# A row tile transposed inside the first Q tile, copied out by two engines, and the second Q tile put ahead of the first K tile

## Chip, cores, metric

One core of one Trainium2 chip. The metric is the device time of one execution in microseconds (us). A run is called fast or slow by its granted clock and its time; only fast runs are compared here.

## The reference

Sequence 2048, width 512. One layer norm feeds two branches that are added to the input: a sliding dilated attention with 32 heads of 16, a window of 8 and a dilation of 2, and a gated feed-forward of inner width 1376.

```python
def _A_ref(x, wqkv, wo):
    ...
    qkv = (lambda x, *d: x.transpose(*d))((x @ wqkv).reshape(B, S, 3, H, Dh), 2, 0, 3, 1, 4)
    ...
    idx = pos[:, None] - off[None, :]          # off = 0, 2, ..., 14
    ...
    logits = jnp.einsum("bhsd,bhswd->bhsw", q, kg) * scale
    logits = jnp.where(mask[None, None, :, :], logits, -1e9)
    attn = _softmax(logits, axis=-1)
    o = jnp.einsum("bhsw,bhswd->bhsd", attn, vg)
    return (lambda x, *d: x.transpose(*d))(o, 0, 2, 1, 3).reshape(B, S, D) @ wo

def _B_ref(x, w_gate, w_up, w_down):
    g = jnp.einsum("bsd,df->bsf", x, w_gate)
    u = jnp.einsum("bsd,df->bsf", x, w_up)
    h = _gelu(g) * u
    return jnp.einsum("bsf,fd->bsd", h, w_down)

xn = _layernorm(x, axis=-1)
return x + _A_ref(xn, A_wqkv, A_wo) + _B_ref(xn, B_w_gate, B_w_up, B_w_down)
```

## The kernel before

The kernel lists every piece of work as a task with an engine, a modelled duration, what it reads and writes, and a priority. A list scheduler written into the kernel then fixes the order on each engine, the buffers and the semaphore waits. So a change of one priority can move instructions everywhere. The sequence is cut into four blocks of 512 rows, each of four row tiles of 128.

Priorities are shifted by group of tasks, and two constants say how much slack the scheduler leaves for TensorE:

```python
SHIFT = {
    "acc0": 361, "acc1": -284, "acc3": -893, "er1": 381, "er2": 159, "er3": -18, "ffn0": 449, "ffn1": -216,
    # ... 30 more
}
SCHED = dict(PE_SLACK=1.6, DMA_BPUS=250e3,
             TOL=dict(pe=0.6, act=-0.3, dve=-0.3, pool=-0.3, sp=0.0))
```

The weights of Q, K and V come in three transfers on the same queue as the input tiles, in the order of their priorities:

```python
t_w = G.task("sp", "ld_w" + nm, 0, mk(), wr=[(I_wq, nm)],
             prio=(-958, -957.5, -898)[i], nbytes=512 * 1024)      # i = q, k, v
```

In block 0 each normalised row tile is transposed by TensorE (`tpx`) and copied out of PSUM. Tile 0 alone is split over two PSUM buffers and copied out by ScalarE (`evx`) and VectorE (`evy`) at the same time (from 5.50 and 5.53 us in the trace); the others are copied by ScalarE alone:

```python
it_tp = Item("tpx" + nm, P_ps, "tp")
it_t2 = Item("tpy" + nm, P_ps, "tp") if nm == "0_0" else it_tp
# ... transposes into it_tp and it_t2
if p == 0 and grp[0] == 0:
    def mk_ev2(it=it_t2, itx=XTI[b], o=o):
        return lambda e: e.tensor_copy(
            out=xnT[:, itx.slot, 2:4, o:o + 128],
            in_=PSB[:, 1024 * it.slot + 256:1024 * it.slot + 512].rearrange("q (k c) -> q k c", k=2))
    t_of["evy" + nm] = G.task("dve", "evy" + nm, d_dve(256), mk_ev2(), rd=[it_t2],
                              wr=[(XTI[b], ("y", p % 2, grp[0]))], prio=-200)
nk = 2 if "evy" + nm in t_of else 4
# ... evx copies the first nk of 4 quarters on ScalarE
```

The Q (`mmt0_t`) and K (`mmt1_t`) tiles of block 0 are 16 matmuls of 128 columns each. Their order on TensorE, and that of VectorE's layer norm steps, is fixed by hand:

```python
chain(["bnst0", "bnag0", "sub0", "rstd0", "norm0", "bnst1", "bnag1", "evy0_0", "sub1", "rstd1", "norm1",
       "bnst2", "bnag2", "sub2", "rstd2", "norm2", "bnst3", "bnag3", "sub3", "rstd3", "norm3", "bnst4"])
# ...
chain(warm_tasks[:len(WARM[0])] + ["tpx0_0"] + warm_tasks[len(WARM[0]):] +
      ["mmt0_0", "tpx0_1", "mmt1_0", "mmt0_1", "tpx1_0", "mmt1_1", "tpx1_1",
       "mmt0_2", "mmt1_2", "mmt0_3", "mmt1_3"])
```

`warm_tasks` are matmuls on zeros that keep TensorE busy while the first tile is normalised (11 in the trace, from 1.25 us on, the last two after tile 0's transposes). After Q, K and V of block 0 (V: 16 matmuls of 512 columns), the attention's elementwise products run on VectorE, and TensorE sums them with narrow, column-tiled matmuls. The logits task `er` begins with 8 matmuls in tiles of 64 columns (the last columns of the up projection) and goes on in tiles of 32 columns; the output sums `pvr` are in tiles of 32 columns alone:

```python
def mk_r(grp=list(er_grp), lg=it_lg, itu=it_u10, itx=XTI[b]):        # er
    def f(e):
        for kt in range(4):
            for c in range(2):
                ins = e.matmul(PS[64 * c:64 * c + 64, ...], lhsT=Wt[:, kt, 128:192], rhs=xnT[...],
                               start=(kt == 0), stop=(kt == 3), tile_position=(0, 64 * c))
        for (g, prs) in grp:
            for wq in range(2):
                for sj in range(4):
                    ins = e.matmul(PS[32 * sj:32 * sj + 32, ...], lhsT=E8[...], rhs=UNI[...],
                                   start=(g == 0), stop=(g == 3), tile_position=(0, 32 * sj))
# ...
                    ins = e.matmul(PS[32 * d4:32 * d4 + 32, ...], lhsT=E4[:, :], rhs=UNI[...],   # pvr
                                   start=(half == 0), stop=(half == 1), tile_position=(0, 32 * d4))
```

Everything else (feed-forward, output projection, accumulation) is ordinary matmuls of 128 to 512 columns.

Of the kernel before, what the change touches and what calls it, by code (L numbers as in the profile page):

```python
# [11 lines left out]
    TOL=dict(pe=0.6, act=-0.3, dve=0.0, pool=0.0, sp=0.0),  # L12
    DMA_ISSUE=0.48,
    DMA_FIXED=2.0,
    DMA_BPUS=330e3,
    ACT_SWITCH=1.35,
    PE_SLACK=0.0,
# [128 lines left out]
class Graph:  # L146
# [466 lines left out]
    def report(self):  # L613
# [11 lines left out]


SHIFT = {
    "acc0": 361, "acc1": -284, "acc3": -893, "er1": 381, "er2": 159, "er3": -18, "ffn0": 449, "ffn1": -216,
    "ffn2": 73, "ffn3": -40, "fin0": -21, "fin1": 305, "fin2": 27, "fin3": -492, "h0": -6, "h1": -944,
    "h2": 606, "ldb1": 326, "ldb2": -35, "ln1": -1581, "ln2": 55, "prod0": 440, "prod1": 888, "prod3": -18,  # L630
    "pv1": -412, "pv2": 970, "pvr0": -976, "pvr1": 126, "pvr2": 463, "qkv1": -43, "qkv2": -1147, "qkv3": -216,
    "sm1": -57, "sm2": -519, "sm3": 750,
}
SCHED = dict(PE_SLACK=1.6, DMA_BPUS=250e3,
             TOL=dict(pe=0.6, act=-0.3, dve=-0.3, pool=-0.3, sp=0.0))

GROUPS = ((r"(?:bnst|bnag|ve|sq|rstd|sub|norm)(\d+)$", "ln", 4), (r"trx(\d+)", "ln", 2),
          (r"(?:mm|evq|evk|evv|stv)(\d)_", "qkv", 1), (r"pr(\d)_", "prod", 1), (r"er(\d)_", "er", 1),
# [29 lines left out]
def bass_parallel_sum__sliding_local_dilated__glu_gated_geglu__prompt_kernel(nc, A_x, A_wqkv, A_wo, B_x, B_w_gate, B_w_up, B_w_down, out, dbg=None, cfg=None):  # L668
# [41 lines left out]
    with contextlib.ExitStack() as es:  # L710
        block = es.enter_context(nc.Block())

        def sb(name, shape, dt):
# [50 lines left out]
        G = Graph()  # L764
        P_ps = Pool("ps", 8, psum=True, quotas=QUOTAS)
# [17 lines left out]
        I_wq = Item("Wqkv")  # L783
# [35 lines left out]
               rd=[I_cf], wr=[I_ident], prio=PC)  # L819
# [10 lines left out]
               rd=[I_E8f], wr=[I_E8], prio=PC2)  # L830
        G.task("pool", "c_zpad", 0.1, lambda e: e.memset(zpad[:, :], 0.0), wr=[I_zpad], prio=PC2)
        G.task("pool", "c_ktpad", 0.15, lambda e: e.memset(KT[:, KTI[0].slot, :, 0:16], 0.0), wr=[(KTI[0], "pad")],
               prio=PC2)
# [9 lines left out]
               rd=[I_E4f], wr=[I_E4], prio=PC2)  # L843
# [4 lines left out]
            rd=[I_mask], wr=[I_mask], prio=PC2 + 10)  # L848
        G.task("act", "c_tbl", 1.5, lambda e: e.activation(
            out=onef[:, 1:2], in_=onef[:, 0:1], func=ACTF.Sqrt),  # L850
            rd=[(I_onef, 0)], wr=[(I_onef, 1)], prio=PC, table="sqrt")
# [3 lines left out]
            rd=[I_zpad], wr=[(I_VD, "pad")], prio=PC + 100, nbytes=512 * 32)  # L855
# [14 lines left out]
        for i, nm in enumerate(("q", "k", "v")):  # L870
            def mk(i=i):
# [4 lines left out]
                         prio=(-958, -957.5, -898)[i], nbytes=512 * 1024)  # L876
# [8 lines left out]
        for (i, src, c0, c1, o) in ((0, B_w_gate, 1280, 1376, 32), (1, B_w_up, 1280, 1312, 0),  # L885
# [9 lines left out]
            wr=[(I_wd, 0)], prio=R_WD, nbytes=1280 * 1024)  # L895
# [13 lines left out]
        t_of = {}  # L909
        XTI = [Item("xt%d" % b, P_xt, "x") for b in range(NB)]  # L910
        for p in range(NP):
# [5 lines left out]
            if p < 2:  # L917
                for t2 in range(2):
                    def mk_ld(t2=t2, p=p, it=it_x):
# [3 lines left out]
                                 prio=((-960, -959), (-957.8, -956.5))[p][t2], nbytes=128 * 1024)  # L923
# [83 lines left out]
            for grp in ((0,), (1,)):  # L1007
                n = len(grp)
                nm = "%d_%d" % (p, grp[0])
                it_tp = Item("tpx" + nm, P_ps, "tp")  # L1010
                it_t2 = Item("tpy" + nm, P_ps, "tp") if nm == "0_0" else it_tp

                def mk_tp(it=it_tp, it2=it_t2, ito=it_x, grp=grp, n=n):
                    def f(e):
                        ins = None
                        for q, t2 in enumerate(grp):
                            for kt in range(4):
                                c0 = 1024 * (it, it2)[kt // 2].slot + kt * 128 * n + q * 128
                                ins = e.transpose(PSB[:, c0:c0 + 128], XIN[:, ito.slot, t2, kt * 128:(kt + 1) * 128],
                                                  ident[:, :])  # L1020
                        return ins
                    return f
                t_tp = G.task("pe", "tpx" + nm, d_mm(128, 4 * n), mk_tp(), rd=[(it_x, t2) for t2 in grp] + [I_ident],
                       wr=[it_tp] if it_t2 is it_tp else [it_tp, it_t2], prio=(-200 if b == 0 else base + 4), mode="f", util=0.5)

                t_tp.urgent = b == 0

                o = 256 * (p % 2) + 128 * grp[0]
                if p == 0 and grp[0] == 0:
                    def mk_ev2(it=it_t2, itx=XTI[b], o=o):  # L1030
                        return lambda e: e.tensor_copy(
                            out=xnT[:, itx.slot, 2:4, o:o + 128],
# [5 lines that stand above are left out]
                def mk_ev(it=it_tp, itx=XTI[b], n=n, o=o, nk=nk):  # L1038
                    return lambda e: e.activation(
                        out=xnT[:, itx.slot, 0:nk, o:o + 128 * n],  # L1040
                        in_=PSB[:, 1024 * it.slot:1024 * it.slot + 128 * nk * n].rearrange("q (k c) -> q k c", k=nk),
                        func=ACTF.Identity)
                t_ev = G.task("act", "evx" + nm, d_act(128 * nk * n), mk_ev(), rd=[it_tp],
                              wr=[(XTI[b], (p % 2, t2)) for t2 in grp], prio=(-200 if b == 0 else base + 6))
                t_of["evx" + nm] = t_ev
                t_of["tpx" + nm] = t_tp
        def chain(names):
            ts = [t_of[q] if isinstance(q, str) else q for q in names]
            for q0, q1 in zip(ts, ts[1:]):
                G.order_after(q1, q0)  # L1050

        chain(["bnst0", "bnag0", "sub0", "rstd0", "norm0", "bnst1", "bnag1", "evy0_0", "sub1", "rstd1", "norm1",
               "bnst2", "bnag2", "sub2", "rstd2", "norm2", "bnst3", "bnag3", "sub3", "rstd3", "norm3", "bnst4"])
        chain(["norm3", "bnst5"])
        chain(["evx0_0", "sq1"])

        QTI = []
        for b in range(NB):
# [7 lines left out]
            if b == 0:  # L1066
                lead = []
                for t in range(4):
                    for which in range(2):
                        it_mm = Item("mmt%d_%d" % (which, t), P_ps, "qkv")  # L1070

                        def mk_mm(which=which, t=t, it=it_mm, itx=XTI[0]):
                            def f(e):
                                ins = None
                                for g in range(4):
                                    for kt in range(4):
                                        ins = e.matmul(  # L1077
                                            PS[:, 512 * it.slot + 128 * g:512 * it.slot + 128 * g + 128],
                                            lhsT=Wqkv[:, kt, which * 512 + g * 128:which * 512 + (g + 1) * 128],
                                            rhs=xnT[:, itx.slot, kt, t * 128:(t + 1) * 128],  # L1080
                                            start=(kt == 0), stop=(kt == 3))
                                return ins
                            return f
                        t_mm = G.task("pe", "mmt%d_%d" % (which, t), 16 * 0.0563, mk_mm(),
                                      rd=[(XTI[0], (t // 2, t % 2)), (I_wq, "qk"[which])]
                                      + ([(XTI[0], ("y", 0, 0))] if t == 0 else []), wr=[it_mm],
                                      prio=-100 + t, mode="f")
                        t_mm.urgent = True
                        t_of["mmt%d_%d" % (which, t)] = t_mm

                        def mk_e(which=which, t=t, it=it_mm, itq=it_qt):
                            def f(e):
                                if which == 0:
                                    o = QT[:, itq.slot, :, t * 128:(t + 1) * 128]
                                else:
                                    o = KT[:, KTI[0].slot, :, 16 + t * 128:16 + (t + 1) * 128]
                                return e.activation(
                                    out=o, in_=PS[:, 512 * it.slot:512 * it.slot + 512].rearrange(
                                        "q (g c) -> q g c", g=4), func=ACTF.Identity)
                            return f  # L1100
                        t_of["ev%s0_%d" % ("qk"[which], t)] = G.task("act", "ev%s0_%d" % ("qk"[which], t), d_act(512), mk_e(), rd=[it_mm],
                               wr=[(it_qt, ("t", t)) if which == 0 else (KTI[0], ("t", t))], prio=-100 + t)
                chain(["evk0_0", "sq3"])
                chain(warm_tasks[:len(WARM[0])] + ["tpx0_0"] + warm_tasks[len(WARM[0]):] +
                      ["mmt0_0", "tpx0_1", "mmt1_0", "mmt0_1", "tpx1_0", "mmt1_1", "tpx1_1",
                       "mmt0_2", "mmt1_2", "mmt0_3", "mmt1_3"])
            for hf in range(nh):
                xparts = [XTI[b]] if nh == 1 else [(XTI[b], (hf, 0)), (XTI[b], (hf, 1))]
                hb = base + (10 * hf if nh > 1 else 0)
# [414 lines left out]
```

## Time and profile before

| | before |
|---|---|
| time, median of 3 runs | 196.44 us (196.17 to 196.82) |
| span of the profiled run | 194.6 us |
| TensorE, VectorE, ScalarE busy | 97%, 79%, 53% |
| V of block 0 starts | 14.53 us |
| first feed-forward matmul | 17.99 us |
| last group of matmuls starts | 191.35 us |

The last three rows are how I read this kernel.

TensorE has no real wait between the V stage and the end, so the time falls into two parts that can be compared apart: **the start** (until V) and **the rest** (first feed-forward matmul to the last group: 191.35 - 17.99 = 173.36). In the views of time shown below, each line has start, duration, engine, line of the kernel, operation, what it writes and reads, and in square brackets the idle time before it and what ended that. A group whose count is one short (15 for 16) has a record missing at its front: 0.22 us of a 512-column matmul are then taken off its start.

### The profile page before, as it was taken

How to read it: one execution, taken by the hardware profiler on the slowest of the kernel's cores; microseconds unless marked ns; L12 is line 12 of the kernel's file. 1: busy time of each engine (PE TensorE's matmuls, PEld its weight loads, DVE VectorE, ACT ScalarE, POOL GpSimd, SP SyncE). 2: the span in 40 equal slices, each digit the busy share in tenths (PEclk: the TensorE clock that was granted, in tenths of full speed). 3: DMA queues.
4: the chain of work that ended last, by engine and by line, in shares of the span. 5: the costliest groups of instructions: out<-in, count | busy, mean ns of one | idle time of the engine just before them, and what ended most of it. 6: DMA issues, size and time to landing. Idle time of an engine off the chain costs nothing.

```text
span 194.6 us, 3228 instructions
## 1 busy us (share of the span) xinstructions
PE 188.5 (97%) x1205; PEld 91.1 (47%) x1224; DVE 153.6 (79%) x240; ACT 104.1 (53%) x171; POOL 8.5 (4%) x31
## 2 busy tenths in 40 slices
PE   7899999999999999999999999999999999999994
PEld 2794444444444443444434444444444444344484
DVE  5989978999799999998999866998974619972132
ACT  3577583776973679701457701764679006586000
POOL 6011001001000000001000100000000000000000
DMA  5999998998723853063657454014970440010121
GB/s 141 352 398 315 312 169 183 263 193 208 185 57 82 220 141 83 18 167 106 162 157 195 58 136 135 27 45 123 245 185 3 108 136 27 0 59 0 44 77 40
DMA packets 34799, 27.03 MB, mean 139 GB/s; under 512 B 11264, under 2 KB 33248, under 8 KB 34784
## 3 DMA queue, kind: packets, MB, share of 16 engines
q1 hardware_dynamic: 34784, 26.83, 54.1%
q8 instruction: 9, 0.15, 0.4%
q14 instruction: 6, 0.05, 0.1%
HBM read 19.99 MB, written 5.26 MB: 130 GB/s over the span
## 4 chain that ended last, share of the span: by engine, by line
PE 81%; DVE 8%; issue 3%; ACT 3%; DMA 3%; SPq 1%; DVEq 0%; ACTq 0%
PE PS L1360 29%; PE PS L1439 19%; PE PS L1123 13%; PE PS L1435 7%; DVE UNI L1308 4%; PE PS L1329 3%; PE PS L1077 3%; PE PS L1207 3%; DMA Wqkv<-in_A_wqkv_dram 3%; PE PS L1395 1%; DVE UNI L1177 1%; ACT UU L1377 1%; PE PS L1200 1%; DVE HT L1382 1%; DVE HT L1410 1%
## 5 line engine op out<-in xcount | busy, mean ns | idle before, releaser
L1439 PE MATMUL PS<-Wd,HT 128*128 128x512 bf16 (+2 forms) x205 | 40.8, 345 | 0.2
L1360 PE MATMUL PS<-xnT,Wu 128*128 128x512 bf16 x154 | 39.6, 379 | 0.6 <-issue 0.5
L1360 PE MATMUL PS<-xnT,Wg 128*128 128x512 bf16 x156 | 39.4, 379 | 0.4 <-issue 0.3
L1308 DVE TENSOR_TENSOR UNI<-BS,PT 128x2048 bf16<-128x2048 bf16 x32 | 37.1, 1219 | 2.9 <-DMA XR<-in_A_x_dram 1.8
L1177 DVE TENSOR_TENSOR UNI<-QT,KT 128x2048 bf16<-128x2048 bf16 x32 | 37.1, 1218 | 0.2
L1377 ACT ACTIVATE UU<-PS 128x512 bf16<-128x512 f32 x40 | 24.0, 601 | 21.2 <-PE PS L1360 21.1
L1123 PE MATMUL PS<-xnT,Wqkv 128*128 128x512 bf16 x155 | 34.8, 379 | 0.5 <-DVE PS L1245 0.2
L1370 ACT ACTIVATE GG<-PS 128x512 bf16<-128x512 f32 x40 | 23.8, 602 | 18.2 <-PE PS L1360 18.1
L1439 PEld LDWEIGHTS PS<-Wd,HT 128*128 128x128 bf16 x209 | 19.6, 98 | 18.5
L1459 DVE TENSOR_TENSOR OB<-PS,XR 128x512 bf16<-128x512 f32 (+2 forms) x19 | 11.5, 605 | 18.3 <-PE PS L1439 18.3
L1360 PEld LDWEIGHTS PS<-xnT,Wg 128*128 128x128 bf16 x160 | 15.3, 98 | 19.6 <-ACT UU L1377 0.8
L1360 PEld LDWEIGHTS PS<-xnT,Wu 128*128 128x128 bf16 x160 | 15.3, 98 | 19.6 <-issue 0.8
L1123 PEld LDWEIGHTS PS<-xnT,Wqkv 128*128 128x128 bf16 x160 | 15.4, 98 | 19.2 <-issue 0.8
L1382 DVE TENSOR_TENSOR HT<-GG,UU 128x512 bf16<-128x512 bf16 x40 | 15.8, 421 | 9.5 <-ACT UU L1377 9.4
L1435 PE MATMUL PS<-Wo,OT 128*128 128x512 bf16 (+2 forms) x76 | 16.9, 345 | 0.1
L1133 ACT ACTIVATE QT<-PS 128x512 bf16<-128x512 f32 x12 | 7.2, 597 | 15.4 <-PE PS L1123 15.4
L1340 ACT ACTIVATE OT<-PS 128x512 bf16<-128x512 f32 x16 | 8.7, 594 | 5.9 <-PE PS L1329 5.8
L1147 ACT ACTIVATE VT<-PS 128x512 bf16<-128x512 f32 x16 | 9.6, 597 | 4.1 <-PE PS L1123 4.1
L937 DVE BATCH_NORM_STATS2 st<-XIN 128x6 f32<-128x512 bf16 x16 | 10.4, 682 | 1.2 <-DMA XIN<-in_A_x_dram 1.2
L1435 PEld LDWEIGHTS PS<-Wo,OT 128*128 128x128 bf16 x76 | 7.2, 98 | 7.0
L1140 ACT ACTIVATE KT<-PS 128x512 bf16<-128x512 f32 x12 | 7.2, 598 | 2.9 <-PE PS L1123 2.9
L1077 PE MATMUL PS<-xnT,Wqkv 128*128 128x128 bf16 x128 | 7.8, 219 | 0.6 <-DMA Wqkv<-in_A_wqkv_dram 0.5
(63 smaller groups left out, 130.9 us busy)
## 6 DMA issues: line engine op xcount, KB each, us to landing
BS<-vt_scratch SPq DMA_DIRECT2D x64, 128.5 KB, 3.0
vt_scratch<-VT SPq DMA_DIRECT2D x16, 128.0 KB
XR<-in_A_x_dram SPq DMA_DIRECT2D x16, 128.0 KB, 2.1
out_dram<-OB SPq DMA_DIRECT2D x14, 128.0 KB, 2.0
Wqkv<-in_A_wqkv_dram SPq DMA_DIRECT2D x3, 512.0 KB, 4.2
XIN<-in_A_x_dram SPq DMA_DIRECT2D x6, 256.0 KB, 7.9
Wg<-in_B_w_gate_dram SPq DMA_DIRECT2D x1, 1280.0 KB
Wu<-in_B_w_up_dram SPq DMA_DIRECT2D x1, 1280.0 KB
```

Of the source, the lines that this page charges most:

```text
L937: return lambda e: e.bn_stats(out=st[:, t, :], in_=XIN[:, it.slot, t2, :])
L1077: ins = e.matmul(PS[:, 512 * it.slot + 128 * g:512 * it.slot + 128 * g + 128], lhsT=Wqkv[:, kt, which * 512 + g * 128:which * 512 + (g + 1 ...
L1123: ins = e.matmul(PS[:, 512 * it.slot:512 * it.slot + HWD], lhsT=lhsT, rhs=xnT[:, itx.slot, kt, c0:c0 + HWD], start=(kt == 0), stop=(kt == 3))
L1177: return lambda e: e.tensor_tensor(out=UNI[:, it.slot, :, :], in0=bass.AP(QT, (itq.slot * 4 + g) * 512, [[NQT * 4 * 512, 128], [0, 4], [1, ...
L1308: return lambda e: e.tensor_tensor(out=bass.AP(UNI, ito.slot * 2048, [[NUNI * 2048, 128], [512, 4], [128, 4], [1, 128]]), in0=bass.AP(BS, ...
L1360: ins = e.matmul(PS[0:M, 512 * it.slot:512 * it.slot + 512], lhsT=Wx[:, kt, j * 128:j * 128 + M], rhs=xnT[:, itx.slot, kt, :], start=(kt = ...
L1370: return lambda e: e.activation(out=GG[0:M, ito.slot, :], in_=PS[0:M, 512 * it.slot:512 * it.slot + 512], func=ACTF.Gelu_apprx_tanh)
L1377: return lambda e: e.activation(out=UU[0:M, ito.slot, :], in_=PS[0:M, 512 * it.slot:512 * it.slot + 512], func=ACTF.Identity)
L1382: return lambda e: e.tensor_tensor(out=HT[0:M, ito.slot, j, :], in0=GG[0:M, ig.slot, :], in1=UU[0:M, iu.slot, :], op=ALU.mult)
L1435: ins = e.matmul(PS[:, 512 * it.slot:512 * it.slot + CW], lhsT=OT[:, ito.slot, dq, ti * 128:(ti + 1) * 128], rhs=Wo[:, dq, c0:c1], start=( ...
L1439: ins = e.matmul(PS[:, 512 * it.slot:512 * it.slot + CW], lhsT=HT[:, ith.slot, j, ti * 128:(ti + 1) * 128], rhs=Wd[:, j, c0:c1], start=Fal ...
L1459: return lambda e: e.tensor_tensor(out=OB[:, ito.slot, 0:CW], in0=PS[:, 512 * it.slot:512 * it.slot + CW], in1=XR[:, itx.slot, c0:c1], op= ...
```

## The change

The intent is to take away TensorE's wait on the K weights: put the Q tile of row tile 1 ahead of the K tile of row tile 0, have tile 1 ready sooner by transposing it inside the first Q tile (after 12 of its 16 matmuls), and shorten its copy-out by giving half to VectorE. All priorities were then tuned anew.

```diff
 SHIFT = {
-    "acc0": 361, "acc1": -284, "acc3": -893, "er1": 381, ...
+    "acc0": 91, "acc2": 150, "acc3": 165, "er0": -90, ...
 }
-SCHED = dict(PE_SLACK=1.6, DMA_BPUS=250e3,
-             TOL=dict(pe=0.6, act=-0.3, dve=-0.3, pool=-0.3, sp=0.0))
+SCHED = dict(PE_SLACK=1.0, DMA_BPUS=250e3,
+             TOL=dict(pe=0.3, act=-0.3, dve=-0.3, pool=-0.3, sp=0.0))
...
-                it_t2 = Item("tpy" + nm, P_ps, "tp") if nm == "0_0" else it_tp
+                it_t2 = Item("tpy" + nm, P_ps, "tp") if p == 0 else it_tp
...
-                if p == 0 and grp[0] == 0:
+                if p == 0:
...
-               "bnst2", "bnag2", "sub2", "rstd2", "norm2", ...
+               "evy0_1", "bnst2", "bnag2", "sub2", "rstd2", "norm2", ...
...
+                        gs = (0, 1, 2, 3)
+                        if t == 0 and which == 0:
+                            t_mm = G.task("pe", "mma0_0", 12 * 0.0563, mk_mm((0, 1, 2)), rd=mrd, wr=[it_mm],
+                                          prio=-100, mode="f")
+                            ...
+                            gs = (3,)
...
-                chain(["evk0_0", "sq3"])
+                chain(["evx0_0", "sq1", "evx0_1", "evq0_0", "sq2"])
+                chain(["evx1_0", "sq3"])
                 chain(warm_tasks[:len(WARM[0])] + ["tpx0_0"] + warm_tasks[len(WARM[0]):] +
-                      ["mmt0_0", "tpx0_1", "mmt1_0", "mmt0_1", "tpx1_0", "mmt1_1", "tpx1_1",
-                       "mmt0_2", "mmt1_2", "mmt0_3", "mmt1_3"])
+                      ["mma0_0", "tpx0_1", "mmt0_0", "mmt0_1", "mmt1_0", "tpx1_0", "mmt1_1", "mmt0_2", "tpx1_1",
+                       "mmt1_2", "mmt0_3", "mmt1_3"])
```

## The prediction

No term of its sum is among them: it still comes to 0.0 for the start, the middle and the end each, 196.4 us. 0.38 and 0.58 to 0.60 us are ScalarE's copies of 256 and 512 columns in the trace, and 0.16 us is the time from the end of a copy to the start of the Q matmul. That a reordering makes no matmul cheaper was the assumption (0.0558 us for 128 columns and 0.863 for a group of four of 512, in the kernel before).

> **What bounds the kernel now.** I read the page first, then the list of waits of TensorE, then the timeline of the first 26 us, then the timelines of TensorE and VectorE over the rest.
>
> From the page of the kernel before, the span and the busy time of each engine:
>
> ```profile
> span 194.6 us, 3228 instructions
> ...
> PE 188.5 (97%) x1205; PEld 91.1 (47%) x1224; DVE 153.6 (79%) x240; ACT 104.1 (53%) x171; POOL 8.5 (4%) x31
> ```
>
> TensorE (PE) is busy almost throughout. The list of waits of TensorE alone (columns: who waited for whom, total us, times, longest) says how little there is to win:
>
> ```profile
> PE PS L863 <- DVE wsrc L812: 1.2, 1, 1.2
> PE PS L1360 <- issue: 0.8, 5, 0.2
> PE PS L1077 <- DMA Wqkv<-in_A_wqkv_dram: 0.5, 1, 0.5
> PE PS L1123 <- DVE PS L1245: 0.2, 1, 0.2
> PE PS L1123 <- issue: 0.2, 1, 0.2
> ```
>
> The first is the start of the program. The only other real wait is 0.5 us for the K weights. The 0.2 us pieces are each one missing record: where they stand, a group of four shows only three matmuls (0.16 us is less than one 0.216 us matmul). The timeline of the start (start, duration, engine, line, operation) shows where the 0.5 us lies:
>
> ```profile
> 4.86 0.61 PE L1019 MATMUL PS<-ident,XIN 128*128 128x128 bf16 x4
> ...
> 5.50 0.38 ACT L1039 ACTIVATE xnT<-PS 128x256 bf16<-128x256 bf16 x1 [1.34 <-PE PS L1019]
> 5.53 0.26 DVE L1031 COPY xnT<-PS 128x256 bf16<-128x256 bf16 x1
> ...
> 6.04 1.05 PE L1077 MATMUL PS<-xnT,Wqkv 128*128 128x128 bf16 x16
> ...
> 6.30 0.35 DVE L993 TENSOR_SCALAR XIN<-XIN,rstd 128x512 bf16<-128x512 bf16 x1
> 6.57 0.69 DVE L937 BATCH_NORM_STATS2 st<-XIN 128x6 f32<-128x512 bf16 x1
> ...
> 6.93 0.39 PE L1019 MATMUL PS<-ident,XIN 128*128 128x128 bf16 x4
> ...
> 7.71 0.58 ACT L1039 ACTIVATE xnT<-PS 128x512 bf16<-128x512 bf16 x1
> ...
> 7.83 1.96 PE L1077 MATMUL PS<-xnT,Wqkv 128*128 128x128 bf16 x32 [0.51 <-DMA Wqkv<-in_A_wqkv_dram]
> ...
> 14.75 3.40 PE L1123 MATMUL PS<-xnT,Wqkv 128*128 128x512 bf16 x15
> ```
>
> The reader is to see: row tile 0 is transposed at 4.86 and copied out of PSUM in two halves (ScalarE 5.50, VectorE 5.53); its Q tile runs at 6.04; tile 1 is transposed at 6.93; then TensorE stands until the K weights land, 7.83. The V stage shows 15 of 16 records, so it began one matmul earlier, 14.75 - 0.22 = 14.53. From 7.83 to 14.53 are 6.70 us for 112 matmuls and 8 transposes of 128 columns, 0.0558 each: no hidden stall in there. From 14.53 to the last matmul (191.35 + 0.78 = 192.13) TensorE has no gap. So the bound is TensorE's own work, plus 6 us of start and about 2.5 us of end.
>
> [...] the trace has 0.38 and 0.58 to 0.60. So halving a copy-out saves ScalarE about 0.2 us, not half. [...] the trace has it between 5.88 (copy ends) and 6.04 (Q matmul starts): 0.16 us, and I charge that for each hand-over from a copy to TensorE.
>
> **The change part by part.** (a) Only 12 of tile 0's 16 Q matmuls precede tile 1's transpose, the other 4 follow. (b) Tile 1's transpose is copied out by ScalarE and VectorE in halves. (c) Tile 1's Q goes before tile 0's K, so the K weights are needed one tile later. (d) The small square roots on ScalarE and the VectorE order are rechained. (e) All priorities and two slack constants are retuned, so the whole schedule is another one. No matmul is added or removed.
>
> Start, with the trace's durations. Nothing before 6.04 changes. Twelve matmuls end at 6.04 + 12 x 0.056 = 6.71; tile 1 is normalised at 6.65, so its transpose starts at 6.75. A copy starts 0.43 after its transpose (10.05 against 9.62 for tile 2), so at 7.18; the half copies end at 7.56 (ScalarE, 0.38) and 7.44. Q of tile 1 may start at 7.56 + 0.16, about 7.70. Meanwhile TensorE does the transpose and the 4 leftover matmuls: 6.75 + 8 x 0.056 = 7.20. So it stands for about **0.45 to 0.5 us**, where it stood 0.51 before: the wait on the K weights (they land near 7.8, needed now near 8.6) becomes a wait on tile 1's copy-out. The restart at 7.70 instead of 7.83 is worth 0.13.
>
> It is given back. VectorE now does tile 1's copy at 7.18 to 7.44 before tile 2's statistics, which started at 6.57: its chain is 0.85 us later. Tile 2 took 1.82 us from statistics to normalised (6.57 to 8.39), so it is ready at 9.25; its transpose comes at 7.70 + 32 x 0.056 = 9.49: just in time. Its copy-out (a full 0.60) runs 9.92 to 10.52, released 10.68; TensorE has one K tile between, done at 9.49 + 20 x 0.056 = 10.61: 0.07 lost. The same distance comes again at tile 3: 0.07. Sum: 7.70 + 6.70 + 0.14 = 14.54 against **14.53** before. The start gains nothing, with perhaps 0.2 us either way.
>
> Middle: the order of instructions shows the same matmuls. Each change between full-array and column-tiled matmuls (L1207, L1329) costs about 0.22 us (0.10 in; out, 98.56 to 99.54 is 0.98 for 0.86 of work). Both orders have 11 such excursions: before, the last logits pass was merged with an output sum; after, the second logits pass is. So nothing there. The question is only whether TensorE now has to wait. VectorE's deadlines, with a 2048-column product at 1.146 us (9.16 for 8) and a 4-matmul group at 0.863:
> - first logits: products start 0.9 later (18.0, not 17.12) and end at 27.2; TensorE arrives two groups sooner, 14.53 + 3.45 + 12 x 0.863 + 0.1 = 28.4. Spare 1.2.
> - second logits: the last product ends near 63 (block 1's products start near 46 after the softmax of block 0 and the normalisation of block 2, with copies of the gated product and four attention products in between), TensorE is there near 67.5: about 4 us spare. Third and fourth: one group sooner than before; about 1.2 each.
> - output sums of blocks 0 to 2: 0.6 to 1.7 spare, worked likewise.
> - output sums of block 3: VectorE starts 0.91 after the accumulations end, as before (160.33 to 161.24); TensorE comes after 7 groups (6.04) where 0.91 + 4 x 1.146 = 5.49 is needed, and again at 6.04 + 1.1 + 3.45 = 10.6 against 10.07. Spare 0.4 to 0.5, the tightest; before it was 168.19 - 165.8 = 2.4 and 171.87 - 170.4 = 1.5.
>
> ScalarE has the same 10 table loads. The end (three half tiles, two quarter tiles) is the same.
>
> Sum: start 0.0, middle 0.0, end 0.0: **196.4 us**.
>
> **The rivals.** First, the wait removed is really gone: if copy-out and hand-over of tile 1 are faster than charged, TensorE would get back up to 0.5 us, 195.9. For: the K weights then have 0.8 us to spare. Against: 0.43 + 0.38 + 0.16 are the trace's own. Second, VectorE becomes the bound in places: the priorities leave less spare, and one miss costs 0.3 to 1 us, 196.7 to 197.5. For: spare of 0.4 us where it was 1 to 2, and the delayed start of VectorE. Against: at 79% it has idle time to catch up, and no deadline above comes out negative. Third, a transfer collides: block 2's input load is issued earlier and some transposing loads later; the earliest-needed weights (up projection, now needed at 21.4, before 23.2) could be late. For: the queue is dense until 25 us. Against: the gate weights' tail, issued after them on the same queue, landed by 20.2 (8.76 + 0.74 + 10.7).
>
> **Range and chances.** Runs of the kernel before differ by 0.65 us (196.17 to 196.82). The gain is capped near 0.5 (the only wait), so a floor of 195.7; upward one missed deadline of 0.5 to 0.8: 197.2. Two per cent is 3.9 us: faster than 192.5 would need less matmul work, which is not there; slower than 200.4 needs five missed deadlines. So 0.01 faster, 0.97 same, 0.02 slower.
>
> **What would show it.** In the changed profile: the wait of Q/K matmuls on the DMA of the weights gone, in its place one of about 0.45 us on the copy-out (xnT) or on VectorE; tile 1's transpose near 6.75; V near 14.5; products of block 0 starting near 18.0; no other TensorE wait over 0.2 us. If TensorE waits on VectorE products, the second rival is right; if V starts at 14.1 or earlier, the first. The prediction is wrong if the time leaves 195.7 to 197.2.

## More of the kernel before

```profile
17.99 5.34 PE L1360 MATMUL PS<-xnT,Wg 128*128 128x512 bf16 x24
...
191.35 0.78 PE L1439 MATMUL PS<-Wd,HT 128*128 128x128 bf16 x11
...
17.94 3.62 PE L1367 MATMUL PS<-xnT,Wg 128*128 128x512 bf16 x16
...
191.42 0.78 PE L1446 MATMUL PS<-Wd,HT 128*128 128x128 bf16 x11
```

The first matmul of a group is what counts; how many follow in one line depends on the stretch that was asked for.

## The result, and the profile after

| | before | after |
|---|---|---|
| time, median of 6 runs of the same rounds | 196.38 us (196.17 to 196.82) | 196.41 us (196.23 to 196.54) |
| span of the profiled run | 194.6 us | 194.7 us |
| V of block 0 starts | 14.53 us | 14.49 us |
| the rest | 173.36 us | 173.48 us |

The ratio is 0.9997, with a 95% interval of 0.9983 to 1.0012. A ratio here is always the mean time of one kernel's fast runs over that of the other's fast runs of the same rounds, so it is not quite the ratio of the medians quoted. The change made no difference that the clock can show.

The waits of TensorE in the kernel after (who waited for whom, us in total, times, longest):

```profile
PE PS L862 <- DVE wsrc L811: 1.2, 1, 1.2
...
PE PS L1076 <- ACT xnT L1038: 0.3, 1, 0.3
PE PS L1076 <- DMA Wqkv<-in_A_wqkv_dram: 0.2, 1, 0.2
```

The wait of 0.5 us on weights has become two: 0.3 us on the copy-out of tile 1, as predicted in kind, and 0.2 us on a weight transfer, which was not predicted. The view of time of the start of the kernel after shows which:

```profile
5.52 0.38 ACT L1038 ACTIVATE xnT<-PS 128x256 bf16<-128x256 bf16 x1 [1.29 <-PE PS L1018]
...
6.25 0.83 PE L1076 MATMUL PS<-xnT,Wqkv 128*128 128x128 bf16 x12 [0.23 <-DMA Wqkv<-in_A_wqkv_dram]
...
6.92 0.39 PE L1018 MATMUL PS<-ident,XIN 128*128 128x128 bf16 x4
...
7.14 0.39 PE L1076 MATMUL PS<-xnT,Wqkv 128*128 128x128 bf16 x4
7.34 0.38 ACT L1038 ACTIVATE xnT<-PS 128x256 bf16<-128x256 bf16 x1 [1.25 <-PE PS L1018]
7.34 0.29 DVE L1030 COPY xnT<-PS 128x256 bf16<-128x256 bf16 x1 [0.67 <-PE PS L1018]
...
7.78 1.96 PE L1076 MATMUL PS<-xnT,Wqkv 128*128 128x128 bf16 x32 [0.25 <-ACT xnT L1038]
...
9.80 1.95 PE L1076 MATMUL PS<-xnT,Wqkv 128*128 128x128 bf16 x32
...
14.71 3.40 PE L1130 MATMUL PS<-xnT,Wqkv 128*128 128x512 bf16 x15
```

Three things are to be seen. First, until 6.25 TensorE waits for the *Q* weights, 0.35 us after tile 0's copy-out ended (5.52 + 0.38 = 5.90). The packed trace also holds the 16 landings of each transfer; the last of them, called the landing here, is at 6.12 for Q, 0.135 us before the first Q matmul. K landed at 7.99 in this run, where it had landed at 7.78 in the profile before. Second, the split copy-out of tile 1 ends at 7.34 + 0.38 = 7.72, and TensorE goes on at 7.78: the hand-over from a copy to TensorE takes 0.06 us. Third, from 7.78 to V at 14.71 - 0.22 = 14.49 pass 6.71 us, which is the 120 instructions of 128 columns at 0.0558 and nothing else: nothing is lost at tiles 2 and 3. K of tile 0 begins 16 matmuls after 7.78, near 8.67, and no wait on it is left.

### The profile page after: what moved, and what is told of

Same layout as the page of the kernel before. It is cut to its first block, busy times and chain, and to the rows that moved or that the text cites. A ratio compares the mean times of both kernels' runs of the same rounds, so it can differ in the third digit from the quotient of the medians.

```text
span 194.7 us, 3220 instructions
## 1 busy us (share of the span) xinstructions
PE 188.9 (97%) x1205; PEld 91.0 (47%) x1224; DVE 153.8 (79%) x241; ACT 104.0 (53%) x171; POOL 9.9 (5%) x31
## 4 chain that ended last, share of the span: by engine, by line
PE 95%; DMA 2%; issue 1%; SPq 0%; ACT 0%; DVE 0%; DVEq 0%
PE PS L1367 35%; PE PS L1446 20%; PE PS L1130 18%; PE PS L1442 7%; PE PS L1336 4%; PE PS L1214 4%; PE PS L1076 4%; DMA Wqkv<-in_A_wqkv_dram 2%; PE PS L1402 2%; PE PS L1207 1%; SPq L919 0%; PE PS L1018 0%; ACT xnT L1038 0%; DVE OB L1466 0%; DVEq L558 0%
## 5 line engine op out<-in xcount | busy, mean ns | idle before, releaser
L1389 DVE TENSOR_TENSOR HT<-GG,UU 128x512 bf16<-128x512 bf16 x40 | 16.3, 423 | 9.1 <-ACT UU L1384 8.6
```

The source lines that it names most:

```text
L1389: return lambda e: e.tensor_tensor(out=HT[0:M, ito.slot, j, :], in0=GG[0:M, ig.slot, :], in1=UU[0:M, iu.slot, :], op=ALU.mult)
```

## The experiments

Since the scheduler reorders everything when a priority moves, every edited kernel below carries the order of each engine and the buffer of each tile as fixed tables, taken from the kernel before or the kernel after, with the named part alone changed. That the tables alone change nothing was not run on the chip; the profiles agree with it in the rest, which is 173.47 or 173.48 with the tables and without them (new order). All twelve results were correct.

My theory, after the result, was: the start exchanges one exposure (K weights) for two others (tile 1's copy-out, Q weights), and gains a little only where the Q weights are in time; the rest does not matter, or costs a little. The rivals: the chain of copy-outs costs back what the order gains (the prediction's own view); the split copy or the swap is idle; the retuned rest eats a real gain of the start.

### One part of the new start undone: k_before_q, whole_copy

```diff
 # k_before_q: the swap of Q and K undone, in the kernel after
-  "mma0_0", "tpx0_1", "mmt0_0", "mmt0_1", "mmt1_0", "tpx1_0", ...
+  "mma0_0", "tpx0_1", "mmt0_0", "mmt1_0", "mmt0_1", "tpx1_0", ...
```

> The changed kernel with one part undone: tile 0's K goes before tile 1's Q again; every other instruction keeps its order, engine by engine, and its buffer. Theory (the start has two waits of nearly equal length, one on the K weights and one on tile 1's copy-out, and the order only chooses which is seen): TensorE waits for the K weights until about 7.8 us, none on the copy-out afterwards, V begins at 14.5 +- 0.1, total within 0.3 us of the changed kernel. Rival (running Q ahead saves the 0.5 us and the rest of the schedule loses it): V begins near 15.0 and the total is 0.5 us longer.

Measured: 196.74 us (196.48 to 197.17), ratio 1.0008 (0.9928 to 1.0087). The wait on the weights is back: 0.44 us, until the K weights let TensorE go on at 7.65. V starts at 14.60, which is 6.95 after that instead of 6.70. The other 0.25 stood between the groups at 9.67: ScalarE's order was frozen, so it evicted Q of tile 1 before it copied tile 2. The time itself is too blurred for 0.1 us (three rounds, and one run of the kernel before at 198.96, with a clock of 0.991, which pulls its mean up; it is in the ratios of the next three runs too). What follows: the swap does take away the wait on K, and this run measures it, but with a side effect of the freezing in it.

```diff
 # whole_copy: ScalarE alone copies tile 1, in the kernel after
-   it_t2 = Item("tpy" + nm, P_ps, "tp") if p == 0 else it_tp
+   it_t2 = Item("tpy" + nm, P_ps, "tp") if nm == "0_0" else it_tp
-   if p == 0:
+   if p == 0 and grp[0] == 0:
-   + ([(XTI[0], ("y", 0, t))] if t < 2 else [])
+   + ([(XTI[0], ("y", 0, t))] if t < 1 else [])
-   chain([... "norm1", "evy0_1", "bnst2", ...
+   chain([... "norm1", "bnst2", ...
```

> The changed kernel with the other part undone: tile 1's transpose is copied out whole by ScalarE (0.58 us) instead of in two halves of 0.38 and 0.29 us; all other orders and buffers frozen. Theory: Q of tile 1 starts 0.2 us later than in the changed kernel, near 8.0 instead of 7.78, V at 14.7 instead of 14.49, and the total is 0.2 us longer, which three rounds hardly resolve; VectorE is up to 0.9 us earlier with tile 2 (statistics at about 6.6 instead of 7.55), and that brings nothing. Rival (VectorE's detour over the copy is what gives the gain back): the total is shorter than the changed kernel's, by 0.3 us or more.

Measured: 196.57 us (196.29 to 196.91), ratio 0.9992 (0.9925 to 1.0059). From tile 1's transposes to the restart pass 7.68 - 6.60 = 1.08 us; in the kernel after it is 7.78 - 6.92 = 0.86. So the split of the copy saves **0.22 us** on the path. It did not show in V (14.39), because in this run everything before it was earlier: TensorE took the first Q matmul at 5.90. That the first Q matmul moves by some tenths from run to run is taken up below.

### The K weights delayed: late_k_before, late_k_after

```diff
 # the K weights are loaded after the V weights, in either kernel
-  prio=(-958, -957.5, -898)[i]
+  prio=(-958, -897.9, -898)[i]
```

> The kernel before with one load moved: the K weights are issued after the V weights, so they land later by one 512 KB load, about 1.4 us at the 354 GB/s that the 5 to 10 us stretch shows; all other orders frozen. Theory: the wait on the K weights grows from 0.5 to about 1.9 us, V begins at about 15.9, and since TensorE has no slack afterwards the whole of it reaches the end: 197.8. Rival (the schedule after the start has slack that swallows it): V late, total under 197.0.

> The same moved load in the changed kernel. Theory (what the change bought is tolerance: the K weights are needed at 8.67 instead of 7.3): a wait of about 0.6 us before the first K matmuls, V at about 15.1, total near 197.0, so 0.8 us less than the kernel before with the same late load, although the two are equal with the load in its place. Rival (the order of Q and K does not matter for the arrival): both lose the same 1.4 us.

Measured: 200.54 us (199.73 to 202.4), ratio 1.0207, for the old start; 198.13 us (197.81 to 200.05), ratio 1.0091, for the new one. The direction is as expected, the distance of 2.4 us is three times the 0.8 expected. TensorE in late_k_before:

```profile
6.94 0.39 PE L1142 MATMUL PS<-ident,XIN 128*128 128x128 bf16 x4
10.27 3.23 PE L1200 MATMUL PS<-xnT,Wqkv 128*128 128x128 bf16 x32 [2.94 <-DMA Wqkv<-in_A_wqkv_dram]
13.30 0.63 PE L1142 MATMUL PS<-ident,XIN 128*128 128x128 bf16 x4
...
18.61 1.67 PE L1246 MATMUL PS<-xnT,Wqkv 128*128 128x512 bf16 x7
```

TensorE could go on with K at 10.27 instead of 7.83, 2.44 us later (1.4 had been assumed). Then 32 matmuls took 13.30 - 10.27 = 3.03 us instead of 1.80. Busy time by stretch (each engine's busy time and count, then the granted TensorE clock, the share of the DMA engines and GB/s) says why:

```profile
10.50:10.75 0.25, 0.25 (x9) 0.25 (x6) 0.00 (x0) 0.00 (x0) 0.00 (x0) 0.93 0.43 148
10.75:11.00 0.25, 0.25 (x6) 0.25 (x4) 0.00 (x0) 0.00 (x0) 0.00 (x0) 0.50 0.24 82
...
14.00:14.25 0.25, 0.25 (x6) 0.25 (x4) 0.25 (x1) 0.25 (x1) 0.00 (x0) 0.75 1.11 410
```

The clock fell to half 0.44 us *after* TensorE had gone on (0.93 over 10.50 to 10.75 puts the step at 10.71), and stayed there until 14.12 (0.75 over 14.00 to 14.25): 3.41 us at half speed. What makes the clock fall, and why for this long, no run here shows; in this run it followed the wait of 2.94 us. The half clock cost another 1.6 us (18.61 - 14.53 = 4.08, of which 2.44 are the transfer), and the whole 4.1 reached the end (span 198.7).

The start of the same run shows two paces too. Its matmuls on zeros reach the full pace early; in the kernel before the same three took longer:

```profile
3.78 0.71 PE L986 MATMUL PS<-wsrc 128*128 128x512 bf16 x3
...
3.78 1.17 PE L863 MATMUL PS<-wsrc 128*128 128x512 bf16 x3
```

The packed trace has their starts at 3.36, 3.78, 4.05 and 4.27, so 0.43, 0.27 and 0.22 us apart. The step to full pace then lies near 3.89 (an estimate: the part of the 0.27 us at the pace of 0.43 is 0.11).

A run with 3.41 us at half clock should show a mean clock of 0.991 (an estimate: 1 - 3.41/2/198.7). All four runs of late_k_before are at 0.991 or below (one at 0.982). Elsewhere single runs at 0.991 that count as fast stand 1.6 to 2.7 us above the median of their kernel (198.96 for the kernel before, 200.05 for late_k_after, 198.21 for q_act_before, 200.23 for sum_early). That each of them lost one such stretch is the guess; they have no profile.

In the profile of late_k_after the waits were short pieces (0.58 on Q, 0.75 on K), the granted clock stayed at 1.00, V came at 15.94 (+1.45), and the span was 196.1 (+1.4). Of the 1.45, 0.52 come from before the restart (7.78 to 8.30: the Q weights were later, and the first Q tile took 0.86 us instead of 0.67), and 0.93 from K, which landed 2.08 later than in the kernel after (10.07 against 7.99).

What follows: a delay of V reaches the end one to one, and the new order needs K late enough to absorb about half of such a delay (1.15 of 2.08). Of the distance between the two starts in V (4.08 - 1.45 = 2.63), 1.6 is the clock and 1.0 the order, near the 0.8 expected. That tolerance is what the change really buys; at the normal landing times it has nothing to absorb but half a microsecond.

### Start and rest apart: start_only, rest_only

```diff
 # start_only: the new start (code, order and buffers) with the old SHIFT and SCHED and the old order of all else
 # rest_only:  the old start with the new SHIFT and SCHED and the new order of all else
```

> The start of the changed kernel with the old order of everything after it. Theory: within 0.3 us of both kernels, V at 14.2 to 14.5 depending on how early the Q weights land in the profiled run. Rival (start saves, retuning loses): 0.5 us shorter than the kernel before.

> The start of the kernel before (its order up to the last K tile of block 0, copies whole) with the retuned order of everything after it taken from the changed kernel, instruction by instruction. Theory (the rest of both schedules keeps TensorE free of waits, so it costs the same): within 0.3 us of both kernels, V at 14.5, no wait of TensorE on VectorE products. Rival (the new start saves 0.5 us and the retuning loses it): 0.5 us longer than the kernel before.

Measured: start_only 196.09 us (195.93 to 196.29) against 196.53 us (196.07 to 197.31, 11 runs) of the kernel before, ratio 0.9971 (0.9952 to 0.9990). rest_only 196.9 us as the median of its five fast runs (196.35 to 198.18; 197.1 with the slow one), ratio of the fast runs 1.0022 (0.9991 to 1.0053); its profiled run was a slow one at 288.44 us and a clock of 0.666, so its profile is not used. TensorE at the start of start_only:

```profile
5.95 0.97 PE L1201 MATMUL PS<-xnT,Wqkv 128*128 128x128 bf16 x12
6.75 0.39 PE L1143 MATMUL PS<-ident,XIN 128*128 128x128 bf16 x4
...
7.61 1.96 PE L1201 MATMUL PS<-xnT,Wqkv 128*128 128x128 bf16 x32 [0.25 <-ACT xnT L1163]
...
14.54 3.40 PE L1255 MATMUL PS<-xnT,Wqkv 128*128 128x512 bf16 x15
```

The Q weights were in time here. Tile 1's transposes begin at 6.75, the very number of the prediction (by luck: 5.95 plus a first Q tile of 0.80 us, where 6.04 plus 0.71 was predicted); the restart is at 7.61, and V at 14.54 - 0.22 = 14.32, **0.21 earlier** than before. So this start is 0.2 us ahead of the one profile of the kernel before.

### The Q weights moved: q_act_before, q_act_after

```diff
 # the Q weights' transfer is issued from ScalarE's queue, after its first activation, instead of SyncE's
+ t_w.on_act = nm == "q"
...
- for t in self.order[eng_name]:
-     if t.on_act:
+ todo = list(self.order[eng_name])
+ if eng_name == "act":
+     todo[1:1] = [t for t in self.order["sp"] if t.on_act]
+ for t in todo:
+     if t.on_act and eng_name == "sp":
          continue
```

> The kernel before with the load of the Q weights issued from ScalarE's queue right after its first activation is queued, instead of third on SyncE's queue; so every later load on SyncE is issued 0.45 us sooner, the K weights too. Theory (the start is limited by the weights' arrival, then by the hand-over chain): the wait on the K weights falls from 0.5 to 0.1 us or less, then the copy-out of tile 1 (ends near 8.3) limits; V at about 14.1, the total 0.3 to 0.4 us shorter. Rival (loads are limited by bandwidth, not by issue): weights land at the same time, tile 0's input later, nothing gained.

> The same edit in the changed kernel. Theory: the K weights are not what it waits for, so only the 0.2 us on the Q weights can be won: V at about 14.2 to 14.3, the total 0.2 us shorter, so no better than the kernel before with the same edit. Rival (with weights early the new order finally pays): 0.5 us or more shorter than the kernel before with the edit.

Measured: 196.57 us (196.27 to 198.21), ratio 1.0023 (0.9986 to 1.0060), with the old start; 196.81 us (196.66 to 196.99), ratio 1.0008 (0.9989 to 1.0026), with the new one. The attempt to have Q sooner missed: tile 1's input landed later (in q_act_before its statistics began at 5.40 instead of 4.73). VectorE's half of tile 0's copy is ordered after them and moved from 5.53 to 6.22, so the first Q matmul came later, not sooner: 6.58 and 6.49, both after a wait on VectorE's copy. V then stands at 14.72 and 15.02. The rival (the queue is full, so what one transfer gains another loses) was right: from 5 to 6 us the transfers moved 381 and 382 GB/s, where it was 384 in the kernel before. The pair shows one thing more. The first Q matmul came 0.54 later than before with the old start and 0.54 later than in start_only with the new one. V moved by 0.19 in the first (14.53 to 14.72) and by 0.70 in the second (14.32 to 15.02; 0.16 of it is a slower first Q tile, 0.96 us instead of 0.80). The old start hides most of a late Q behind its wait on K; the new one does not.

### All four combinations on one chip: after_again, start_only_2, rest_only_2

```diff
 # the kernels after, start_only and rest_only again, unchanged, five rounds each on the same chip
```

> The changed kernel unaltered, to see how its start moves from run to run. Theory (the new start depends on when the Q weights land, which in its first profile was 0.2 us late, and not on the K weights): V begins at 14.3 if the Q weights land before 5.95, later one for one if not; the total within 0.3 us of the kernel before.

> New start with the old rest, again, on the same chip as the changed kernel. Theory (the new start is worth 0.2 us when the Q weights are in time, the new rest costs about 0.1 us): 0.1 to 0.3 us shorter than the changed kernel, V at about 14.3. Rival (start and rest are both worth nothing, the first result was chance): equal to the changed kernel within 0.1 us.

> Old start with the new rest, again, because its first profile fell in a throttled run. Theory: 0.1 to 0.3 us longer than the kernel before; from the first matmul on Wg to the end 176.7 us, as in the changed kernel, where the kernel before has 176.6. Rival: no difference to the kernel before.

| | median us (range) | ratio (95%) | V | the rest |
|---|---|---|---|---|
| before (old start, old rest) | 196.40 (196.04 to 196.82, 10 fast runs) | 1 | 14.53 | 173.36 |
| start_only_2 (new, old) | 196.01 (195.93 to 196.37) | 0.9979 (0.9966 to 0.9992) | 14.28 | 173.36 |
| rest_only_2 (old, new) | 196.38 (196.27 to 196.66) | 0.9996 (0.9983 to 1.0008) | 14.48 | 173.48 |
| after_again (new, new) | 196.36 (196.15 to 196.61) | 0.9994 (0.9981 to 1.0007) | 14.68 | 173.47 |

(V and the rest of the first row are from the first profile of before; the other rows are from their own.) start_only wins again, at a second chip: it is the best version, 0.2% to 0.3% ahead of the kernel before and outside the noise, though far inside 2%.

**Why the start of after_again gained nothing.** Its Q weights were in time, yet V came at 14.68:

```profile
5.93 1.35 PE L1076 MATMUL PS<-xnT,Wqkv 128*128 128x128 bf16 x12
7.11 0.39 PE L1018 MATMUL PS<-ident,XIN 128*128 128x128 bf16 x4
...
7.97 1.96 PE L1076 MATMUL PS<-xnT,Wqkv 128*128 128x128 bf16 x32 [0.25 <-ACT xnT L1038]
```

From 5.93 to 7.11 are 1.18 us for 12 matmuls that take 0.67 at the full pace of 0.056. TensorE was still at about half that pace until about 7.0: in the packed trace the starts are 0.106 us apart up to 6.97, and 0.056 from 7.06. Other runs reach full pace sooner. In sum_early (below) the first transposes, at 4.73, already last 0.39 us instead of 0.61. In the runs here the step to full pace lies between about 3.9 us (late_k_before, above) and about 7.1 us (q_act_after, an estimate: from 6.49 to 7.45 are 0.96 us for 12 matmuls, 0.29 more than at full pace, so about six of them took 0.106); what sets it is not shown. With the new start the first Q tile lies on the path, so its pace counts. With the old one up to half a microsecond of it is hidden in the wait on K.

Put together, the profiles follow two simple sums. Old start: V comes 6.70 after the first K matmul (7.83 to 14.53; 7.77 to 14.48 in rest_only_2). New start: V comes 8.24 or 8.25 after the first Q matmul if TensorE is at full pace by then (6.25 to 14.49; 6.03 to 14.28), later by what is left of the half pace (5.95 to 14.32: 8.37; 5.93 to 14.68: 8.75). The first Q matmul itself came at 5.81 to 6.25 in the runs with the usual order of transfers (at 6.58 in late_k_after, where only K had moved). What moves the landing of the Q weights from run to run is not known: the transfers ahead of them are the same.

Comparing two single profiles is therefore not fair to either order, and the landings allow a better reading. The old order starts 0.05 us after K has landed (7.78 to 7.83 before, 7.72 to 7.77 in rest_only_2) and has V 6.70 later, so each run with the new start also says where the old one would have had V (an estimate: landing of K + 6.75):

| | K landed | V, old order (estimate) | V, new order (measured) | gain |
|---|---|---|---|---|
| after | 7.99 | 14.74 | 14.49 | 0.25 |
| after_again | 7.68 | 14.43 | 14.68 | -0.25 |
| start_only | 8.09 | 14.84 | 14.32 | 0.52 |
| start_only_2 | 7.74 | 14.49 | 14.28 | 0.21 |
| sum_early | 7.53 | 14.28 | 14.05 | 0.23 |

So in the first profile of the kernel after the new start did gain: every transfer was 0.2 late there, K too. My theory, that it gains only where the Q weights are in time, does not hold. It lost in one run of the five, the one with the late full pace.

**Why the rest costs 0.12.** The rest is 173.35 or 173.36 in five profiles with the old order (before, late_k_before, start_only twice, q_act_before), and 173.47 or 173.48 in seven with the new one. So it lies in the order, not in the run. Both orders run a logits task and an output sum back to back once, which saves a change from column-tiled to ordinary matmuls and back (0.12 and 0.10 us where the kernel before has both around one output sum, 98.46 to 99.54). Before, the logits of block 3 come first and the output sum after:

```profile
134.09 1.91 PE L1207 MATMUL PS<-UNI,E 128*32 128x512 bf16 x32
135.82 1.04 PE L1329 MATMUL PS<-UNI,E 128*32 128x512 bf16 x16
137.02 0.81 PE L1360 MATMUL PS<-xnT,Wu 128*128 128x512 bf16 x3 [0.16 <-issue]
```

After, the output sum of block 0 comes first and the logits of block 1 after:

```profile
66.30 1.05 PE L1336 MATMUL PS<-UNI,E 128*32 128x512 bf16 x16
67.28 0.63 PE L1207 MATMUL PS<-xnT,Wt 128*64 128x256 bf16 x8
67.83 1.91 PE L1214 MATMUL PS<-UNI,E 128*32 128x512 bf16 x32
```

Sixteen such matmuls are 0.86 us of work, 32 are 1.73 (in the trace they start four at a time, 0.216 us apart). Before, the step from logits to sum is free (135.82 - 134.09 = 1.73). After, the step from the sum to the logits costs 0.12 (67.28 - 66.30 = 0.98), since the logits task opens with tiles of 64 columns (`128*64` in the record), and the change from tiles of 32 to tiles of 64 is paid. That is the 0.12 by which the rest is longer. Its size and place match; a kernel with the pair turned round alone was not run.

**What stays open.** By the times, the means of the fast runs of the four combinations on this chip are 196.45, 196.08, 196.40 and 196.38 us. The new start is worth 0.37 with the old rest and only 0.03 with the new rest; two gains that simply add up would not do this. The profiles explain part of it (0.12 of the rest; the late pace in after_again's one profile), but each profile is one run, and the starts of the other runs are not recorded. Whether the remainder is chance (each ratio is known to about ±0.26 us) is not settled.

### A deadline of VectorE missed on purpose: sum_early

```diff
 # kernel after: TensorE's first output sum of block 3 three groups earlier
-  fg3_1 fu3_1 fg3_2 fu3_2 fg3_3 fu3_3 fg3_4 pvr3_1 fu3_4 ...
+  fg3_1 fu3_1 fg3_2 fu3_2 pvr3_1 fg3_3 fu3_3 fg3_4 fu3_4 ...
```

> The changed kernel with the first output sum of block 3 moved three 4-matmul groups (2.59 us) earlier on TensorE, nothing else moved: a deadline of VectorE missed on purpose. Theory (spare at this place is the 0.6 us that the trace shows, and after a miss nothing catches up): TensorE waits 2.59 - 0.6 = 2.0 us on VectorE's products there, and the total is 2.0 us longer, 198.4. Rival (the later groups take up the wait, because ScalarE and the second sum have slack): total under 197.4.

Measured: 198.23 us (198.05 to 200.23), ratio 1.0122 (1.0080 to 1.0165), 1.9 us over after_again. TensorE, and below it VectorE, in two views of the same run:

```profile
162.55 1.03 PE L1491 MATMUL PS<-xnT,Wu 128*128 128x512 bf16 x4
165.63 1.05 PE L1460 MATMUL PS<-UNI,E 128*32 128x512 bf16 x16 [2.06 <-DVE UNI L1439]
```

```profile
160.87 9.16 DVE L1439 TENSOR_TENSOR UNI<-BS,PT 128x2048 bf16<-128x2048 bf16 x8
```

The fourth product ends at 160.87 + 4 x 1.145 = 165.45, and TensorE goes on 0.18 later. The rest of this run is 193.10 - 17.50 = 175.60, which is 2.12 over the 173.48 of the kernel after: the whole wait reaches the end, and nothing later takes it back. In the kernel after, the same sum runs at 166.54, with its four products done at 161.31 + 4 x 1.146 = 165.89: 0.65 us to spare. So the retuned order runs closer to this deadline than the old one did (2.4 us), and it does hold.

## Why the prediction was right

**The number.** 196.4 was predicted, 196.41 measured. It is right partly by luck, because errors of the steps cancelled, so the steps are gone through.

**What bounds the kernel**: confirmed. Late K weights (+4.1 us) and a missed deadline (+2.1 us) both reached the end whole; TensorE has nothing to give back.

**The wait changes hands**: right in kind. In the kernel after, the wait on K is gone and one on tile 1's copy-out stands there. It is 0.25 us in the record, not 0.45 to 0.5. From the end of work, start to start, TensorE stood from 7.36 to 7.78, 0.42; before, it stood from 7.15 to 7.83, 0.68, which the record shows as 0.51. I had set a start-to-start figure beside a recorded one.

**The hand-over of 0.16 us from a copy to TensorE**: this is the term that was mis-sized. It measures 0.06 (5.87 to 5.93 in after_again, 7.72 to 7.78 in after) and 0.05 (7.56 to 7.61 in start_only). The 0.16 had been read from one place, 5.88 to 6.04, before the first Q matmul; that place also needs the Q weights, and in the run before they landed at 5.91, after the copy. The first Q matmul follows the landing of its weights by 0.135 us (0.13 to 0.14) in seven runs (before, after, late_k_before, late_k_after, start_only_2, rest_only_2, sum_early), so there the transfer was the releaser, not the copy.

**"It is given back" (0.07 at tile 2 and 0.07 at tile 3)**: wrong. No such gap is in any run of the new start with its own order. It followed from the same 0.16: with 0.06 tile 2's copy is released at 10.58, and TensorE is there at 10.61. With the right term the prediction's own sum gives 7.56 + 0.05 + 6.70 = 14.31 for V. start_only measures 14.32 (with the luck at 6.75 said above).

**What took the gain instead**: in the first profile of the kernel after, transfers 0.21 later than in the profile before (Q and K alike, so the old order would have lost as much); in after_again, a late full pace; and 0.12 in the rest. The prediction took the time before 6.04 as unchanged and did not see that the new start lays it open. Its third rival, a transfer that comes late, is the nearest, but it had looked at the up projection, where nothing happened.

**The middle**: "so nothing there" was wrong by 0.12. Counting 11 excursions on each side was right; that the saved change is worth less when the output sum comes first was missed.

**VectorE's deadlines**: held, and well. The products of block 0 started at 17.85 (18.0 predicted), the first logits task began at 28.40 (28.4), the spare of block 3's sum was 0.65 (0.4 to 0.5). The second rival, VectorE as the bound, is excluded for this kernel; sum_early shows what it would have looked like. The first rival, the wait really gone, is half true: 0.2 us are to be had, in start_only.

## What to carry to other kernels

Where one engine is busy throughout, a reordering at the start is worth at most the wait that it takes away, and it may lay open what that wait had hidden: ask what each run-to-run variation (a transfer's landing, the moment of full pace) does to the old order and to the new one. Measure the cost of a hand-over at a place where only that hand-over can be waited for, before adding it up over a chain. Where a trace holds the landings, ask of one and the same run what the other order would have done with them, since two profiles differ by more (0.2 us here) than the change is worth. When a change has a local idea and a global retuning in it, time both halves apart: here the idea alone was 0.2% to 0.3% faster, and with the retuning there was nothing.

## What the traces show of single costs

- After a wait of TensorE of 2.94 us (late_k_before) the clock was at half from 10.71 to 14.12, and fell only after TensorE had gone on. That cost 1.6 us on top of the 2.44 by which K came later. The profile of sum_early, with a wait of 2.06 us, has a mean clock of 0.999, and that of late_k_after, with waits of 0.58 and 0.75, one of 1.00.
- The step to full pace lay between about 3.9 us (late_k_before) and about 7.1 us (q_act_after) of the span (estimates, from the starts above).
- The granted clock in the records does not show that first half pace. In after_again it reads 1.00 from 6.00 to 7.00, while 12 matmuls of 128 columns took 1.18 us instead of 0.67.
- From the end of a ScalarE copy to the start of the matmul that needs it: 0.05 to 0.06 us (start_only, after). From a VectorE product to a column-tiled matmul: 0.18 us (sum_early; whether the change of tiling is in it is not shown). From the landing of a transfer to the matmul that needs it: 0.135 us for the Q weights, 0.04 to 0.05 for the K weights (5.91 to 6.04 and 7.78 to 7.83 in the kernel before); why they differ is not known.
- A change of tiling: 0.10 us from ordinary matmuls to tiles of 64 or 32 columns (30.07 to 30.17 and 98.46 to 98.56 in the kernel before), 0.12 back (99.42 to 99.54), 0.12 from tiles of 32 columns to tiles of 64 (67.16 to 67.28 in the kernel after), and nothing seen from a logits task to a sum that both use tiles of 32 (135.82 - 134.09 = 1.73 us for eight fours 0.216 apart).
